# Unread products behind the transpositions of batch 0's last pair, the mix's factors loaded as rows, and w_r's second half loaded ahead of v's last pair

## The chip, the cores and the metric

One core of one Trainium2 chip runs the whole program. The metric is the device time of one execution in microseconds (us), lower is better. Before the change it is 579.75 us, the median of three runs (578.79 to 580.51).

## The reference

Three layers follow one another, in float32. A windowed attention (4 batches, 8 heads, 576 positions, head width 64; a window of 32, dilated by 4 in the upper four heads), a channel mix with a shifted input, and a mixture of four attention experts.

```python
scores = scale * np.matmul(q, k.transpose(0, 1, 3, 2))
scores = np.where(masks[None, :, :, :], scores, -1000000000.0)
attn = softmax(scores)
x = np.matmul(attn, v)                      # to [B, S, 512]
...
xk = mu_k * x + (1.0 - mu_k) * x_prev       # x_prev: x one position earlier
xr = mu_r * x + (1.0 - mu_r) * x_prev
k = np.maximum(xk @ w_k, 0.0)
v = k * k @ w_v
r = 1.0 / (1.0 + np.exp(-(xr @ w_r)))
x = r * v
...
# per expert: q, k, v = x @ wq[e], x @ wk[e], x @ wv[e]; causal softmax; @ wo[e]; top 2 of 4 summed
```

## The kernel before, in words

**Batch 0's attention.** The heads are worked in four pairs (`hp` 0 to 3). `load_qk` loads a pair's q and k, `turn_qk` turns them on TensorE (L241) and copies them out (L260 on VectorE for q, L262 on ScalarE for k). `attn_weights` makes the masked scores in two parts of five and four blocks of 64 queries (`sc`, L289 for the mask, L296), takes the rows' extreme (L309), the exponentials (L319, ScalarE) and the normalisation (L323 to L325, VectorE). `attn_values` goes over three thirds: three transpositions of the weights into a PSUM bank `pt` (L353), a copy out of it (`pts`, L354, ScalarE), then the products with v into `av` (L363). `pt` has two banks, `av` one. After four and a half blocks the result goes to the tile `x` (L378, ScalarE), which frees `av`.

**The mix.** `mix_feature` forms, for feature block f (the pair's 128 features) and each half c of the positions, `m` (L481 on ScalarE, L482 on VectorE) and splits it in a high and a low part, `xh` (L484) and `xl` (L485). The factors mu and 1-mu lie in `mus`; `load_mus` loads them with two DMAs of single 4-byte elements (L108, L109) and forms 1-mu on VectorE (L110).

**Products in three passes.** `product` (L506) multiplies high by high, low by high and high by low, so each output has 12 products (four feature blocks by three). `z` is the receptance (w_r, copied by L514), `h` the keys (w_k, L520 and after: `kh`, `kl`), `v` the values (w_v). Four output blocks fo by two halves c: `z_0_2` is c = 0, fo = 2. These share three banks (`mm`).

**Weights.** `load` fetches a part of w_r (2 parts), w_k (4) or w_v (4) raw; `split_cols` splits it: L631 (ScalarE) and L633, L634 (VectorE) on the raw words, then the high part L639 (ScalarE) and the low part L640 (VectorE). Outputs 0 and 1 of `z` need w_r's part 0, outputs 2 and 3 its part 1. Raw tiles lie in buffers of other things: w_k's part 2 and w_v's parts 1 and 3 share one buffer with the v windows (`vw`) of batch 1.

**What sets the order.** Each engine has one queue, worked front to back. A framework lays the queues out when the program is built: it follows the order of the code, but moves an instruction ahead where its own estimate says that it is ready earlier. `tc.keep_in_program_order` pins an instruction. `keep_warm` issues products of a zero tile that nobody reads (512 columns, L76), 16 at the start and one after each step of batch 0's attention. All loads named here go through one DMA queue, SP's, except pair 2's v (GpSimd's queue).

**After batch 0's attention** the layers of batch 0 start (`dbatch`: all `z`, then `h`, then `v`), and batch 1's attention is interleaved with them from about 88 us on. The later batches follow the same pattern, then the experts.

Of the kernel before, what the change touches and what calls it, by code (L numbers as in the profile page):

```python
# [8 lines left out]
F32 = mybir.dt.float32  # L9
# [12 lines left out]
def tile_dilated_attention__rwkv_channel_mix__moe_attention(  # L22
# [37 lines left out]
    def ps(tag, name):  # L60
        return psum["pool"].tile([128, 512], F32, tag=tag, name=name, bufs=psum[tag])
# [9 lines left out]
    def keep_warm(n):  # L71


        p = ps("mm", "idle")
        for _ in range(n):
            nc.tensor.matmul(p, still[:, :128], still, start=True, stop=True)  # L76

    keep_warm(16)

    def band(name, base, p1=0, j1=0):  # L80
# [4 lines left out]
        for h in range(2):  # L85
# [5 lines left out]
            if j1:  # L91
# [11 lines left out]
    nc.gpsimd.affine_select(out=tri, in_=tri, pattern=[[1, E], [-1, E]], base=-1,  # L103
                            channel_multiplier=0, compare_op=ALU.is_ge, fill=0.0)
    mus = cpool.tile([128, 2, 2, KT], F32, name="mus")

    def load_mus():
        nc.sync.dma_start(mus[:, 0, 0, :], mu_k.rearrange("(c p) -> p c", p=128))  # L108
        nc.sync.dma_start(mus[:, 0, 1, :], mu_r.rearrange("(c p) -> p c", p=128))  # L109
        nc.vector.tensor_scalar(out=mus[:, 1], in0=mus[:, 0], scalar1=-1.0, scalar2=1.0, op0=ALU.mult, op1=ALU.add)  # L110

    X = {}
# [34 lines left out]
    def load_qk(ap, dp, b, hp):  # L147

        dil = hp >= NP // 2
        qk = []
        if b == 0:
            if hp % 2 == 0:
                early["raw"] = dp.tile([128, 8, 512], F32R, tag=("wv_hi", "wv_lo")[hp // 2], name=f"rqk_{hp}",
                                       bufs=1).bitcast(F32).rearrange("p k f -> p (k f)")
            for n, src in enumerate((q, k)):
                c = 768 * (2 * (hp % 2) + n)
                r = early["raw"][:96, c : c + 768].rearrange("p (s h d) -> p s h d", h=2, s=6)
                nc.sync.dma_start(r, src[b, 2 * hp : 2 * hp + 2].rearrange("h (a s) d -> a s h d", s=6))  # L160
                qk.append(r)
            return qk
        for n, (src, nm) in enumerate(((q, "q"), (k, "k"))):
            if "rawall" not in early:
                early["rawall"] = ap.tile([128, 4, 18, 32], F32, tag="raw", name="rqk", bufs=1)
            r = early["rawall"][:, (2 * (hp % 2) if b == 1 else 0) + n]
            for j in range(2):
                for g in range(2):
                    nc.sync.dma_start(
                        r[j * 64 + g * 32 : j * 64 + g * 32 + 32],  # L170
                        src[b, 2 * hp + j].rearrange("(c t) (g e) -> g t c e", t=32, e=32)[g],
                    )
            qk.append(r)
        return qk
# [168 lines left out]
    def attn_values(ap, b, hp, vw, pe=None, pT=None):  # L343

        dil = hp >= NP // 2
        nm = f"{b}_{hp}"
        av = None
        for i in range(3):
            if pT is None:
                pt = ps("pt", f"pt_{nm}_{i}")  # L350
                pts = ap.tile([WK, 384], F32, tag="pts", name=f"pts_{nm}_{i}", bufs=2)
                for a in range(3):
                    nc.tensor.transpose(pt[:WK, 128 * a : 128 * a + 128], pe[:, 3 * i + a, :], ident)  # L353
                nc.scalar.copy(pts, pt[:WK, :384])  # L354
            for a in range(3):
                t = 3 * i + a
                cuts = [(0, 64)] if t != 4 else [(0, 32), (32, 64)]
                for u0, u1 in cuts:
                    p0 = QB * t + u0
                    if p0 in (0, 288):  # L360
                        av = ps("pt" if pT is not None and p0 else "av", f"av_{nm}_{p0}")
                    for j in range(2):
                        nc.tensor.matmul(  # L363
                            av[64 * j : 64 * j + 64, p0 % 288 : p0 % 288 + u1 - u0],
                            vw[:, j, t, :],
                            (pts[:, 128 * a + 64 * j + u0 : 128 * a + 64 * j + u1] if pT is None
                             else pT[:, 2 * j + u0 // 32 : 2 * j + u1 // 32, t, :]),
                            start=True, stop=True,
                        )
                    p1 = QB * t + u1  # L370
                    if p1 in (288, 576):
                        hf = p1 // 288 - 1
                        if dil:
                            dst = X[b][:, hp, 1 : S + 1].rearrange("p (i r) -> p r i", r=4)
                            dst, src = dst[:, 2 * hf : 2 * hf + 2, :], av[:, :288].rearrange("p (r i) -> p r i", r=2)
                        else:
                            dst, src = X[b][:, hp, 1 + 288 * hf : 289 + 288 * hf], av[:, :288]
                        nc.scalar.copy(dst, src)  # L378
            if (hp, i) == (NP - 1, 2):
                complete.add(b)  # L380
            yield

    def attn_batch(ap, dp, dq, b):
        new_x(b)
        if b == 0:

            qk = [load_qk(ap, dp, b, 0)]
            vw = [load_v(ap, b, 0)]
            qk.append(load_qk(ap, dp, b, 1))
            vw += [load_v(ap, b, 1), load_v(ap, b, 2)]  # L390
            qk += [load_qk(ap, dp, b, 2), load_qk(ap, dp, b, 3)]
            load_mus()
            load("r", 0)
            vw.append(load_v(ap, b, 3))
            load("r", 1)
            load("k", 0)
            masks_of_first(dp)
            begin_mix(dp, dq, 0, 0)
            begin_mix(dp, dq, 0, 1)
        else:  # L400
            qk, vw = [], []
        for hp in range(NP):
            with tc.issue_after(marks["v2" if hp == 0 else "window"]) if b == 1 and hp < 2 else ExitStack():
                while len(qk) < min(hp + 2, NP):
                    qk.append(load_qk(ap, dp, b, len(qk)))
                while len(vw) < min(hp + 2, NP):
                    vw.append(load_v(ap, b, len(vw)))
            yield from attn_pair(ap, b, hp, (qk[hp], vw[hp]))
            if b == 0:
                mix_feature(0, 0, 1, hp)  # L410
                mix_feature(1, 1, 1, hp)
                if hp == 0:
                    with tc.issue_after(marks["first weights"]):
                        masks_of(1)
# [198 lines left out]
    with tc.tile_pool(name="apool", bufs=2, side="left") as ap:  # L613
# [31 lines left out]
        def load(x, i):  # L645
            pool, src, kts, cols = specs[x]
            if x not in wts:
                wts[x] = tuple(pool.tile([128, kts, cols], F32R, tag=f"w{x}_{h}", name=f"w{x}_{h}") for h in ("hi", "lo"))
            raws[x, i] = load_cols(src, kts, i, {"r": "hl", "k": "3RV1", "v": "RV1V"}[x][i])
# [440 lines left out]
```

## Time and profile before

| | |
|---|---|
| runs, median of 3 | 579.75 us (578.79 to 580.51) |
| profiled execution | 577.75 us, its span 576.0 us |
| instructions | 12510 |
| TensorE (PE) busy | 546.4 us, 95% |
| VectorE (DVE) busy | 344.4 us, 60% |
| ScalarE (ACT) busy | 338.1 us, 59% |
| TensorE's granted clock, mean | 0.986 |

The profile gives, per engine, the time in which instructions ran; the granted clock is TensorE's, 1.00 for 2.4 GHz and 0.50 for 1.2 GHz. A view by stretches shows where in the span an engine is short of work; a timeline gives each instruction's start and length, and in brackets how long the engine had been idle before it and what released it. The instructions named PE are products and transpositions; SPq is the issue of DMAs on SP's queue.

### The profile page before, as it was taken

To read this page: it belongs to the slowest core of one execution; us is meant where nothing else is said; L and a number is where in the kernel's file an instruction comes from. 1 tells how busy PE (TensorE), PEld (TensorE's weight loads), DVE (VectorE), ACT (ScalarE), POOL (GpSimd) and SP (SyncE) were. 2 spreads that over 40 slices of the span, in tenths; PEclk is the share of its full clock that TensorE was granted. 3 is DMA by queue.
4 is the path that set the end of the run, shared out by engine and by line. 5 is a ranking of instruction groups with operands and counts; after the bars stand their busy time and mean duration, and the time that the engine had idled before them with its cause. 6 is when DMAs were issued, how large, how long until landed. Compare 5 with 4: busy or idle time off the path is not lost.

```text
span 576.0 us, 12510 instructions
## 1 busy us (share of the span) xinstructions
PE 546.4 (95%) x4668; PEld 490.8 (85%) x4668; DVE 344.4 (60%) x1112; ACT 338.1 (59%) x968; POOL 79.6 (14%) x101
## 2 busy tenths in 40 slices
PE   8978978899999999999999999999997999999985
PEld 4757968789999999999999999998985988989763
DVE  4567989666657388185262425428577557556662
ACT  4799978465776167285163534227566657665761
POOL 8400000000341032120011403003003003000000
PEclk9996999899999999999999999999999999999999
DMA  9987286755545553131000320054614425416202
GB/s 165 188 304 196 74 206 138 131 105 107 132 107 125 134 109 78 63 94 56 8 1 1 73 75 2 1 125 102 147 26 99 137 62 124 116 46 160 93 1 92
DMA packets 131213, 57.66 MB, mean 100 GB/s; under 512 B 110976, under 2 KB 118224, under 8 KB 131152
## 3 DMA queue, kind: packets, MB, share of 16 engines
q1 hardware_dynamic: 130736, 56.41, 41.3%
q8 instruction: 37, 0.61, 0.4%
q0 software_dynamic: 416, 0.44, 0.4%
q14 instruction: 24, 0.20, 0.1%
HBM read 34.42 MB, written 10.03 MB: 77 GB/s over the span
## 4 chain that ended last, share of the span: by engine, by line
PE 74%; DVE 9%; SPq 7%; ACT 5%; DMA 4%; issue 1%; DVEq 0%; ACTq 0%
PE v L506 17%; PE h L506 12%; PE z L506 7%; PE pv L817 5%; PE av L964 5%; PE pk L506 4%; PE pt L938 4%; PE po L1001 4%; PE pq L506 4%; PE av L363 3%; PE sc L296 3%; PE sc L891 2%; PE sc L893 2%; SPq L160 2%; SPq L182 2%
## 5 line engine op out<-in xcount | busy, mean ns | idle before, releaser
L506 PE MATMUL h<-xh,wk_hi 128*128 128x288 f32 x256 | 77.6, 304 | 4.4 <-ACT r L520 4.4
L506 PE MATMUL v<-kh,wv_hi 128*128 128x288 f32 x256 | 76.2, 302 | 0.4 <-DVE x L536 0.4
L506 PE MATMUL h<-xl,wk_hi 128*128 128x288 f32 x256 | 75.9, 297 | 0.2 <-DVE xl L485 0.2
L506 PE MATMUL v<-kl,wv_hi 128*128 128x288 f32 x256 | 75.9, 299 | 0.0
L506 PE MATMUL h<-xh,wk_lo 128*128 128x288 f32 x256 | 75.3, 294 | 0.0
L506 PE MATMUL v<-kh,wv_lo 128*128 128x288 f32 x256 | 75.3, 296 | 0.0
L903 ACT ACTIVATE pe<-pe,st 128x64 f32<-128x64 f32 (+4 forms) x80 | 44.9, 562 | 19.2 <-DVE st L897 18.0
L520 ACT ACTIVATE r<-h 128x288 f32<-128x288 f32 x64 | 25.9, 407 | 51.3 <-PE h L506 40.8
L496 POOL TENSOR_TENSOR xl<-m,xh 128x1152 fp32r<-128x1152 f32 x12 | 32.0, 2664 | 163.6 <-DMA vw<-in_v_dram 57.4
L506 PEld LDWEIGHTS h<-xh,wk_hi 128*128 128x128 f32 x256 | 48.0, 188 | 7.0 <-ACT r L520 5.6
L897 DVE CUSTOM_DVE_ANT_0 pe<-sc,cmask 128x64 f32<-128x64 f32 (+4 forms) x80 | 33.4, 427 | 31.4 <-PE sc L893 30.4
L506 PEld LDWEIGHTS v<-kh,wv_hi 128*128 128x128 f32 x256 | 48.0, 189 | 1.4 <-DVE x L536 0.6
L506 PEld LDWEIGHTS h<-xl,wk_hi 128*128 128x128 f32 x256 | 48.1, 188 | 0.8 <-DVE xl L485 0.7
L506 PEld LDWEIGHTS v<-kl,wv_hi 128*128 128x128 f32 x256 | 48.3, 189 | 0.4
L506 PEld LDWEIGHTS v<-kh,wv_lo 128*128 128x128 f32 x256 | 48.3, 189 | 0.2
L506 PEld LDWEIGHTS h<-xh,wk_lo 128*128 128x128 f32 x256 | 48.2, 188 | 0.0
L482 DVE SCALAR_TENSOR_TENSOR m<-x,mus,m 128x288 f32<-128x288 f32 x64 | 30.3, 509 | 27.1 <-ACT m L481 27.0
L319 ACT ACTIVATE pe<-pe,st 128x96 f32<-128x96 f32 x108 | 39.1, 364 | 5.8 <-DVE st L315 5.7
L536 DVE SCALAR_TENSOR_TENSOR x<-z,v 128x288 f32<-128x288 f32 x32 | 14.3, 453 | 43.5 <-PE v L506 43.4
L730 POOL TENSOR_TENSOR yl<-x,yh 128x576 fp32r<-128x576 f32 x16 | 21.0, 1344 | 139.1 <-ACT yh L729 73.7
L506 PE MATMUL z<-xh,wr_hi 128*128 128x288 f32 x128 | 39.3, 310 | 0.8 <-ACT z L514 0.8
L530 DVE TENSOR_TENSOR kl<-r,kh 128x288 fp32r<-128x288 f32 x48 | 31.7, 663 | 12.9 <-ACT kh L528 12.6
(176 smaller groups left out, 1473.6 us busy)
## 6 DMA issues: line engine op xcount, KB each, us to landing
kk<-kh SPq DMA_DIRECT2D x32, 144.0 KB, 2.6
kl<-kl SPq DMA_DIRECT2D x32, 144.0 KB, 2.7
raw_in_moe_w_k_dram<-in_moe_w_k_dram SPq DMA_DIRECT2D x4, 1024.0 KB, 9.9
raw_in_moe_w_v_dram<-in_moe_w_v_dram SPq DMA_DIRECT2D x4, 1024.0 KB, 5.8
out_dram<-ob SPq DMA_DIRECT2D x16, 256.0 KB, 2.7
rqk<-in_q_dram SPq DMA_DIRECT2D x48, 72.0 KB, 2.9
rqk<-in_k_dram SPq DMA_DIRECT2D x48, 72.0 KB, 2.7
moved<-turned SPq DMA_DIRECT2D x8, 432.0 KB, 3.1
```

The costliest lines, as they stand in the source:

```text
L319: nc.scalar.activation(pe[:, t, :], pe[:, t, :] if b else sc[:, c0 : c0 + WK], AF.Exp, bias=st[:, 0, t : t + 1], scale=-1.0, accum_out=st[ ...
L482: nc.vector.scalar_tensor_tensor(out=m, in0=x, scalar=mus[:, 0, w, f : f + 1], in1=m, op0=ALU.mult, op1=ALU.add)
L496: nc.gpsimd.tensor_sub(lo, m, hi.bitcast(F32))
L506: nc.tensor.matmul(o, w[:, kt, wsl], x[:, kt, :], start=(n == 0), stop=(n == last))
L520: nc.scalar.activation(r, p, AF.Relu)
L530: half.tensor_sub(kl[:, fo, :], r, kh[:, fo, :].bitcast(F32))
L817: nc.tensor.matmul(p, x[:, kt, t0 : t0 + tn], w[:, kt, 512:772], start=(n == 0), stop=(n == 3 * KT - 1))
L897: nc.vector.tensor_tensor_reduce(out=pe[:tn, PO[t] + c0 : PO[t] + c1], in0=sc, in1=m, scale=-0.125, scalar=(BIG if i == 0 else st[:tn, 1, ...
L903: nc.scalar.activation(pb, pb, AF.Exp, bias=st[:tn, 0, t : t + 1], scale=-1.0, accum_out=st[:tn, 2, t : t + 1])
L938: nc.tensor.transpose(pt[:kn, c0 : c0 + tn], pe[:tn, PO[t] + k0 : PO[t] + k0 + kn], ident[:tn, :tn])
L964: ins = nc.tensor.matmul(av1[p0 : p0 + 64, q0 - 64 : 512], vh[:kn, kb, :], w[i][:kn, c0 : c0 + S - q0], start=(kb == 0), stop=(kb == NB - 1))
L1001: nc.tensor.matmul(p, x[:, t0 : t0 + tn], w[:, g, :], start=(n == 0), stop=(n == 5))
```

## The change

Four edits. `keep_warm_in` issues unread products of 128 columns into the last quarter of the `pt` bank, pinned: eight behind each copy out of `pt` in batch 0's last pair, and sixteen behind that pair's last products. `load_mus` now loads both factors as eight rows of 128 elements, on ScalarE's DMA queue and at the program's head; `turn_mus` turns them on TensorE (into an `av` bank), copies them on VectorE and forms 1-mu. w_r's second half is loaded right behind its first, ahead of v's pair 3.

```diff
+    def keep_warm_in(p, n):
+        for _ in range(n):
+            tc.keep_in_program_order(nc.tensor.matmul(p[:, 384:512], still[:, :128], still[:, :128], start=True, stop=True))
...
     mus = cpool.tile([128, 2, 2, KT], F32, name="mus")
+    rows = cpool.tile([2 * KT, 128], F32, name="rows")
 
     def load_mus():
-        nc.sync.dma_start(mus[:, 0, 0, :], mu_k.rearrange("(c p) -> p c", p=128))
-        nc.sync.dma_start(mus[:, 0, 1, :], mu_r.rearrange("(c p) -> p c", p=128))
+        for w, mu in enumerate((mu_k, mu_r)):
+            nc.scalar.dma_start(rows[KT * w : KT * w + KT, :], mu.rearrange("(c p) -> c p", p=128))
+
+    def turn_mus():
+        p = ps("av", "mus")[:, : 2 * KT]
+        nc.tensor.transpose(p, rows, ident[: 2 * KT, : 2 * KT])
+        nc.vector.tensor_copy(mus[:, 0], p.rearrange("p (w c) -> p w c", w=2))
         nc.vector.tensor_scalar(out=mus[:, 1], in0=mus[:, 0], scalar1=-1.0, scalar2=1.0, op0=ALU.mult, op1=ALU.add)
...
                 nc.scalar.copy(pts, pt[:WK, :384])
+                if (b, hp) == (0, NP - 1):
+                    keep_warm_in(pt, 8)
...
             if (hp, i) == (NP - 1, 2):
                 complete.add(b)
+                if b == 0:
+                    keep_warm_in(pt, 16)
...
+            load_mus()
             qk = [load_qk(ap, dp, b, 0)]
+            turn_mus()
...
-            load_mus()
             load("r", 0)
+            load("r", 1)
             vw.append(load_v(ap, b, 3))
-            load("r", 1)
             load("k", 0)
```

The edits also change the framework's estimates, and with them the queues far behind the edited code. Three places follow.

TensorE's queue where batch 0's last pair ends and its receptance begins (`av_3_288` are the pair's products for the positions from 288 on, `z_0_0` to `z_0_2` the receptance's first outputs). Before:

```order
L363 MATMUL av_3_0_761<-pts_3_1_776,vw_3_251 64x32 x2
L363 MATMUL av_3_288_786<-pts_3_1_776,vw_3_251 64x32 x2
L363 MATMUL av_3_288_786<-pts_3_1_776,vw_3_251 64x64 x2
L363 MATMUL av_3_288_786<-pts_3_2_794,vw_3_251 64x64 x6
L506 MATMUL z_0_0_848<-xh_0_0_276,wr_hi 128x288
L506 MATMUL z_0_0_848<-xl_0_0_277,wr_hi 128x288
```

Now:

```order
L524 MATMUL z_0_2_925<-xh_0_0_280,wr_lo 128x288
L524 MATMUL z_0_2_925<-xh_0_0_280,wr_hi 128x288
L378 MATMUL av_3_288_806<-pts_3_1_788,vw_3_257 64x32 x2
L378 MATMUL av_3_288_806<-pts_3_1_788,vw_3_257 64x64 x2
L378 MATMUL av_3_288_806<-pts_3_2_814,vw_3_257 64x64 x6
L82 LDWEIGHTS still
L82 MATMUL pt_3_2_813<-still 128x128
```

Eleven of the receptance's products, the first of them `z_0_0<-xh_0_0,wr_hi`, now stand ahead of `av_3_288`, and the sixteen unread ones behind it.

ScalarE's queue at the same place (`x<-av_3_0` and `x<-av_3_288` are the copies of the pair's results, the second CAST `wr_hi` is w_r's part 0). Before:

```order
L354 COPY pts_3_2_794<-pt_3_2_793 96x384
L378 COPY x_211<-av_3_0_761 128x2x144
L639 CAST wr_hi<-raw_in_moe_w_r_dram_249 128x4x256
L484 CAST xh_0_0_276<-m_0_0_275 128x288
L378 COPY x_211<-av_3_288_786 128x2x144
L481 ACTIVATE m_0_0_275<-x_211,mus 128x288 x2
L484 CAST xh_0_0_276<-m_0_0_275 128x288
L484 CAST xh_1_1_278<-m_0_0_275 128x288
L481 ACTIVATE m_0_0_275<-x_211,mus 128x288
L484 CAST xh_1_1_278<-m_0_0_275 128x288
L631 ACTIVATE raw_in_moe_w_k_dram_269<-raw_in_moe_w_k_dram_269 128x1024
```

Now:

```order
L657 CAST wr_hi<-raw_in_moe_w_r_dram_253 128x4x256
L502 CAST xh_0_0_280<-m_0_0_279 128x288
L393 COPY x_212<-av_3_0_773 128x2x144
L499 ACTIVATE m_0_0_279<-x_212,mus 128x288
L393 COPY x_212<-av_3_288_806 128x2x144
L502 CAST xh_1_1_282<-m_0_0_279 128x288
L499 ACTIVATE m_0_0_279<-x_212,mus 128x288
L502 CAST xh_0_0_280<-m_0_0_279 128x288
L499 ACTIVATE m_0_0_279<-x_212,mus 128x288
L532 ACTIVATE z_0_891<-z_0_0_892 128x288
L532 ACTIVATE z_0_891<-z_0_1_906 128x288
L649 ACTIVATE raw_in_moe_w_k_dram_674<-raw_in_moe_w_k_dram_674 128x1024
```

The copy `x<-av_3_0` now stands behind w_r's part 0, and the first work on w_k behind the copies of `z_0_0` and `z_0_1`.

TensorE's queue where batch 0's keys end and its values begin (`h_1_7` is the last of the keys, `pt_0_0` the transpositions of batch 1's first pair). Before:

```order
L506 MATMUL h_1_7_1468<-xh_1_3_995,wk_lo 128x288
L353 MATMUL pt_0_0_1349<-ident,pe_0_1285 96x128 x3
L353 MATMUL pt_0_1_1380<-ident,pe_0_1285 96x128 x3
L363 MATMUL av_0_0_1355<-pts_0_0_1350,vw_1274 64x64 x3
L353 MATMUL pt_0_2_1396<-ident,pe_0_1285 96x128 x3
L353 MATMUL pt_1_0_1506<-ident,pe_1_1442 96x128 x3
L506 MATMUL v_0_0_1519<-kh_0_1013,wv_hi 128x288
```

Now:

```order
L524 MATMUL h_1_7_1512<-xl_1_3_1040,wk_hi 128x288
L524 MATMUL h_1_7_1512<-xh_1_3_1039,wk_lo 128x288
L524 MATMUL v_0_0_1563<-kh_0_1057,wv_hi 128x288
L524 MATMUL v_0_0_1563<-kl_0_1058,wv_hi 128x288
L524 MATMUL v_0_0_1563<-kh_0_1057,wv_lo 128x288
L524 MATMUL v_0_0_1563<-kh_0_1057,wv_hi 128x288
```

Twenty-one products of `v_0_0` now follow `h_1_7` directly; batch 1's `pt_0_0` comes behind them, and its `av_0_0` behind another 24 value products. On ScalarE the copy of `h_1_5` (L520), which frees a bank of `mm`, moves from behind the second pair's nine exponentials to ahead of them; on VectorE `kl_0_7` moves ahead of that pair's normalisation.

## Rows read from the trace of the kernel before

**Rows 1.** The page's head: span, and busy time of each engine.

```profile
span 576.0 us, 12510 instructions
PE 546.4 (95%) x4668; PEld 490.8 (85%) x4668; DVE 344.4 (60%) x1112; ACT 338.1 (59%) x968; POOL 79.6 (14%) x101
```

**Rows 2.** Windows: stretch, busy us per engine, granted clock (PEclk), DMA share, GB/s.

```profile
36.00:40.00 4.00, 1.74 (x30) 1.38 (x30) 2.45 (x7) 3.70 (x20) 0.00 (x0) 1.00 1.05 393
...
44.00:48.00 4.00, 2.23 (x30) 1.98 (x29) 3.21 (x4) 3.80 (x7) 0.00 (x0) 0.50 1.03 305
...
64.00:68.00 4.00, 4.00 (x32) 4.00 (x31) 4.00 (x7) 4.00 (x10) 0.00 (x0) 1.00 0.41 119
...
100.00:104.00 4.00, 1.28 (x10) 0.64 (x8) 3.42 (x12) 3.56 (x15) 0.00 (x0) 0.89 0.59 133
104.00:108.00 4.00, 4.00 (x24) 3.95 (x24) 2.19 (x5) 1.90 (x5) 0.00 (x0) 0.69 1.20 191
...
280.00:320.00 40.00, 40.00 (x328) 39.53 (x327) 15.65 (x31) 17.89 (x38) 8.03 (x3) 1.00 0.00 1
```

**Rows 3.** Timeline, 17 to 28 us: SP's queue, VectorE, TensorE, ScalarE.

```profile
17.80 1.99 SPq L108 DMA_DIRECT2D mus<-in_moe_mu_k_dram  x1
19.83 0.76 SPq L109 DMA_DIRECT2D mus<-in_moe_mu_r_dram  x1
...
24.60 0.17 DVE L110 TENSOR_SCALAR mus<-mus 128x8 f32<-128x8 f32 x1 [1.94 <-DMA mus<-in_moe_mu_r_dram]
...
26.83 0.65 DVE L309 TENSOR_REDUCE st<-sc 128x5 f32<-128x480 f32 x1
...
24.06 1.04 PE L296 MATMUL sc<-kT,qT 64*64 64x96 f32 x20
...
24.87 0.53 ACT L481 ACTIVATE m<-x,mus 128x288 f32<-128x288 f32 x1 [1.22 <-DVE mus L110]
```

**Rows 4.** Timeline of ScalarE, the last pair's end.

```profile
7.78 1.18 ACT L262 COPY kT<-kt 128x384 f32<-128x384 f32 x2 [5.69 <-PE kt L241]
...
40.29 0.47 ACT L354 COPY pts<-pt 96x384 f32<-96x384 f32 x1 [0.46 <-PE pt L353]
...
45.90 1.14 ACT L639 CAST wr_hi<-raw_in_moe_w_r_dram 128x1024 fp32r<-128x1024 f32 x1
...
47.56 0.70 ACT L378 COPY x<-av 128x288 f32<-128x288 f32 x1 [0.20 <-PE av L363]
...
51.84 1.20 ACT L631 ACTIVATE raw_in_moe_w_k_dram<-raw_in_moe_w_k_dram 128x1024 f32<-128x1024 f32 x1
```

**Rows 5.** Timeline of TensorE: batch 0's last pair and the receptance.

```profile
32.50 1.04 PE L76 MATMUL idle<-still 128*128 128x512 bf16 x4
...
42.45 0.91 PE L363 MATMUL av<-pts,vw 96*64 96x64 f32 x12 [0.85 <-ACT x L378]
...
46.18 1.33 PE L363 MATMUL av<-pts,vw 96*64 96x32 f32 x20 [1.76 <-ACT x L378]
...
48.09 0.44 PE L506 MATMUL z<-xh,wr_hi 128*128 128x288 f32 x1
48.34 0.44 PE L506 MATMUL z<-xl,wr_hi 128*128 128x288 f32 x1
```

**Rows 6.** Timeline of TensorE, keys to values; then ScalarE, VectorE and SP's queue there.

```profile
99.49 0.71 PE L353 MATMUL pt<-ident,pe 128*96 128x128 f32 x5
...
101.11 0.32 PE L353 MATMUL pt<-ident,pe 128*96 128x128 f32 x1 [0.91 <-DVE pe L325]
...
103.57 0.47 PE L363 MATMUL av<-pts,vw 96*64 96x64 f32 x2 [0.86 <-DMA vw<-in_v_dram]
...
105.14 0.59 PE L506 MATMUL v<-kh,wv_hi 128*128 128x288 f32 x1
...
102.71 0.41 ACT L520 ACTIVATE r<-h 128x288 f32<-128x288 f32 x1
...
103.06 0.45 DVE L530 TENSOR_TENSOR kl<-r,kh 128x288 fp32r<-128x288 f32 x1
```

## The prediction

> **What bounds the kernel now.** Start with the page's head [rows 1]: TensorE is busy 95% of 576.0 us, the two other engines under 60%. So the end moves only where TensorE is short of work or slow. The windows [rows 2] show where: from 280 to 320 us it is busy 40.00 of 40, so nothing is to be had there, while 36 to 40 us has 1.74 of 4, 44 to 48 us 2.23 at a granted clock of 0.50 (1.2 GHz), and 100 to 104 us 1.28. Between these, at 64 to 68 us, VectorE and ScalarE are both busy 4.00 of 4: there they set the pace, and a delay of theirs is passed on. The timelines then tell what TensorE waits for: around 25 us the factors of the mix [rows 3], from 40 to 52 us ScalarE's queue [rows 4, 5], from 99 to 105 us batch 1's attention [rows 6].
>
> All sums are made against the profiled execution, 577.75 us (span 576.0 and 1.75 around it). The median of the runs, 579.75, is 2.00 above it; I carry the difference over to that median. A difference under 0.3% (1.74 us) can't be told from none here.
>
> **Part 1, the factors as rows.** Removed: two DMAs of single elements, 1.99 and 0.76 us of SP's queue [rows 3]. Every later SP transfer moves up by some 2.7 us; w_r's second half also moves past the 13 transfers of v's pair 3, which then come one w_r transfer later than that. None of these is waited for: the pair's products at 42.45 wait for ScalarE, not for a DMA [rows 5]. So the moved half itself counts 0; that cover would be gone only if the pair ran many us earlier. Added: two issues on ScalarE's queue (no row shows one; from 0 to SP's 1.99 each), hidden in the 5.69 us for which ScalarE is idle before 7.78 [rows 4]; a transposition of 8 columns, and one small copy on VectorE like L110's 0.17, both about 7 to 9 us, where VectorE still waits for the first scores. Together 0.
>
> What goes is the wait: VectorE stood 1.94 us and ScalarE 1.22 us for the factors [rows 3]. Late next are the scores of pair 2: their products end at 25.10 (24.06 + 1.04), but VectorE's reduction L309, queued behind the mix, starts only at 26.83. Bounds: 0, if ScalarE's queue is held there otherwise, and 1.73. ScalarE is nearly always busy from there to 40 us, so the shift should be passed on: I take **-1.6**.
>
> **Part 2, the unread products.** Four of 512 columns took 1.04 us at the full clock [rows 5], so 0.065 for 128 columns. At 1.2 GHz two receptance products of 288 columns start 0.25 apart (48.09, 48.34), so 0.11 for 128. Bounds are 0.065 and 0.25; I take 0.11, since the stage runs at 0.50. The Trainium skill (TensorE: Matmul & The Clock Gate, "Back-to-back issue gap") gives about 81 ns for a 128-column product with its weight load; by it, an estimate, sixteen would be 1.3 us instead of the 1.8 below; no row of the kernel before has such a product.
>
> The three groups of eight (0.9 us each) lie in TensorE's waits of 0.85 and 1.76 us [rows 5] and cost 0; without that cover they would cost 2.6. But they stand behind ScalarE's copy out of the same bank and can't start before it. Do they hold the clock? In the rows it was still 1.00 from 36 to 40 us, when TensorE was busy 1.74 of 4, and 0.50 by 44 [rows 2]. The first group follows the copy that begins at 40.29 [rows 4], so the empty stretch ahead of it stays empty. I take it that the clock falls as before and comes back somewhat earlier. The Trainium skill (PSUM — Partial Sum Buffer, "PSUM bank collisions raise a hardware error") forbids TensorE to write into a bank while another engine reads it, disjoint columns included; no row shows it by itself. By that rule the free part of the bank is no place to work during the copy, and the sum is the forecast's; without it the products would fill the copies' time too, and the sum would lie towards the first rival's.
>
> **Part 3, the order at the pair's end.** Here the queues of the change matter. Today ScalarE copies `x<-av_3_288` at 47.56 [rows 4]. Now eleven receptance products stand on TensorE ahead of `av_3_288`; the first waits for w_r's part 0, whose cast ended at 47.04 (45.90 + 1.14) and now comes one copy (0.5) sooner, 46.6. Eleven by 0.25 make 49.3, `av_3_288` at its 1.33 [rows 5] 50.6: the copy comes 3.0 us later (at the full clock, 11 by 0.122, as 328 in 40 us [rows 2], and half of 1.33: 48.6, 1.0 later). Queued behind it on ScalarE are the rest of the mix and, behind the copies of `z_0_0` and `z_0_1`, the first work on w_k. These wait for sixteen unread products (1.8) and 21 of the receptance (2.6 to 5.2), so 4.4 to 7.0 after `x`; ScalarE's own steps to there take about as long as now from 47.56 to the mix's end at 51.84, 4.3. Added wait 0.1 to 2.7; I take 0.9, because the clock should return in this stretch. As ScalarE and VectorE are full later [rows 2], this is passed on: **+3.9** (bounds +1.1 and +5.7).
>
> **Part 4, the order at 99 to 107 us.** Today TensorE finishes the keys at 99.5, then stands behind batch 1's transpositions and products: it waits for the normalisation (0.91), later for `vw` (0.86), and begins the values only at 105.14 [rows 6]. It loses 2.72 us of the window from 100 to 104 (4 - 1.28), and at a mean clock of 0.69 another 1.24 from 104 to 108 [rows 2]: 3.96 us. Now 21 products of `v_0_0` follow the keys directly, 2.6 us at 0.122, and the transpositions follow when their data is there. `v_0_0` needs a free bank, today freed by L520 at 102.71, now ahead of nine exponentials; and its last three products need `kl_0_7`, today 103.06 [rows 6], now ahead of a normalisation. Bounds: 0, if these come no earlier, and -3.96. I take **-3.6**, near the far end, since both releases come sooner and the 2.6 us of products cover the rest of the way; 0.4 is left for a short wait.
>
> Sum: -1.6 + 3.9 - 3.6 = **-1.3 us**: 576.45 for the profiled execution, **578.45** on the runs' scale. That is no change that can be told.
>
> **The rivals.**
>
> *The clock stays up, or returns before the receptance starts.* For it: 24 products more in a stretch with only a few us of waits. Against it: the emptiest part lies ahead of the first group. Then part 3 costs 1.0 for the copy and some 0.4 behind it: -1.6 + 1.4 - 3.6 = -3.8, **575.95**.
>
> *Slower: part 4 gives nothing.* The values' first products wait on TensorE for a bank and `kl_0_7` as long as it waits now for batch 1's attention, because VectorE, full before 104 us (3.42 of 4 even there), delivers both late. Place: TensorE's queue behind `h_1_7`. It decides if `kl_0_7` comes more than 2.6 us behind the keys' end; each us beyond costs one, up to 3.96. Then -1.6 + 3.9 = +2.3, **582.05**. For it: the low parts come late in VectorE's queue today. Against it: both were moved ahead of 2 to 3 us of other work.
>
> *Later waits.* The queues are laid out anew up to some 300 us; batch 2's products now stand ahead of some of batch 1's receptance. If TensorE waits there for the weights' way through memory, 1 to 2 us come on top: about **580**. Against it: TensorE waits for nothing in such stretches now [rows 2].
>
> *The delay of part 3 is absorbed* by VectorE's and ScalarE's short waits between 76 and 100 us: -5.2, **574.55**. Against it: both are full before.
>
> **How the numbers follow.** Forecast 0.47, its own range 577.0 to 580.1 (part 3 from +2.4 to +5.5); clock held 0.23; part 4 gives nothing 0.17; later waits 0.09; absorbed 0.04. The range 575.3 to 581.7 takes in the first, most of the second and the fourth, and half of the third. Faster than 578.0: nearly all of the second and fifth case and four tenths of the forecast, 0.42. Slower than 581.5: most of the third, a little of the others, 0.16. The rest is 0.42.
>
> **What would show it.** Right: the wait for the factors is gone and pair 2's reduction starts near 25.1; the granted clock is near 0.50 when the receptance starts; ScalarE is idle two or three us before `x<-av_3_288`; TensorE goes from keys to values without a gap over 0.5 us, and the clock doesn't fall there. Wrong: a clock of 1.00 from 44 to 48 us; a wait of TensorE ahead of `v_0_0`'s last products; a wait over 1 us between 110 and 300 us.

## The result and the profile after

The changed kernel takes **583.81 us**, median of four runs (583.01 to 583.86), beside 579.50 for the kernel before (578.79 to 580.51) on the same chip: ratio **1.0056, 95% interval 1.0038 to 1.0075**. It is slower by 3.2 us (2.2 to 4.3), more than the 0.3% that can be told from no change. The forecast was 578.45, range 575.3 to 581.7. The profiled execution took 583.01 (span 581.3).

The page's head, against [rows 1]:

```profile
span 581.3 us, 12598 instructions
PE 553.7 (95%) x4706; PEld 495.9 (85%) x4709; DVE 346.0 (60%) x1113; ACT 337.7 (58%) x968; POOL 79.6 (14%) x101
```

TensorE is busy 7.3 us longer, so this is not only idle time: the 40 unread products are some 2.6 us of it (an estimate from the starts in the section on the prediction: eight at 0.107 us, 32 at 0.055), and some of its work ran slower or later. The windows, columns as in [rows 2]:

```profile
36.00:40.00 4.00, 1.85 (x37) 1.51 (x36) 2.58 (x6) 3.48 (x19) 0.00 (x0) 1.00 1.05 402
40.00:44.00 4.00, 4.00 (x37) 3.10 (x38) 3.05 (x6) 3.41 (x6) 0.00 (x0) 0.57 0.96 323
44.00:48.00 4.00, 2.70 (x34) 2.34 (x32) 3.66 (x4) 3.80 (x7) 0.00 (x0) 1.00 1.11 345
48.00:52.00 4.00, 4.00 (x55) 3.77 (x54) 2.13 (x6) 2.33 (x5) 0.00 (x0) 1.00 0.84 188
52.00:56.00 4.00, 4.00 (x31) 3.80 (x30) 1.19 (x3) 3.28 (x7) 0.00 (x0) 1.00 0.62 140
...
92.00:96.00 4.00, 2.52 (x43) 2.09 (x41) 1.57 (x4) 0.00 (x0) 0.00 (x0) 1.00 0.77 197
96.00:100.00 4.00, 2.17 (x10) 2.17 (x11) 3.69 (x15) 3.65 (x10) 0.00 (x0) 0.78 0.47 77
100.00:104.00 4.00, 4.00 (x46) 3.84 (x46) 3.58 (x18) 4.00 (x18) 0.00 (x0) 0.79 0.54 89
```

Three things stand out. The granted clock is 1.00 from 44 to 48 us, where it was 0.50. TensorE is full from 48 to 56 us, but VectorE does only 3.32 us of work in these eight; in the same two windows of the kernel before it did more than twice that:

```profile
48.00:52.00 4.00, 4.00 (x19) 4.00 (x18) 3.06 (x8) 3.12 (x8) 0.00 (x0) 0.51 0.76 171
52.00:56.00 4.00, 3.42 (x26) 3.18 (x25) 3.90 (x7) 4.00 (x8) 0.00 (x0) 1.00 0.68 154
```

And ScalarE does nothing at all from 92 to 96 us; after that the clock falls, while the gap of [rows 2] from 100 to 104 us is filled. The stretch from 92 to 108 us as a whole, before and now:

```profile
92.00:108.00 16.00, 12.72 (x110) 11.57 (x109) 12.29 (x44) 13.17 (x48) 0.00 (x0) 0.89 0.69 117
```

```profile
92.00:108.00 16.00, 12.69 (x130) 11.98 (x129) 12.84 (x59) 11.62 (x46) 0.00 (x0) 0.89 0.63 128
```

TensorE is short of work as long as before: the gap has moved, it has not gone.

The pair's end in ScalarE's timeline, against [rows 4]:

```profile
40.59 0.47 ACT L367 COPY pts<-pt 96x384 f32<-96x384 f32 x1 [0.62 <-PE pt L366]
...
45.70 1.18 ACT L657 CAST wr_hi<-raw_in_moe_w_r_dram 128x1024 fp32r<-128x1024 f32 x1
...
47.06 0.73 ACT L393 COPY x<-av 128x288 f32<-128x288 f32 x1
...
49.44 0.69 ACT L393 COPY x<-av 128x288 f32<-128x288 f32 x1 [0.36 <-PE av L378]
...
53.85 1.13 ACT L649 ACTIVATE raw_in_moe_w_k_dram<-raw_in_moe_w_k_dram 128x1024 f32<-128x1024 f32 x1
```

The copy `x<-av_3_0` stands behind the cast of w_r's part 0 and starts at 47.06; TensorE needs the bank that it frees. So `x<-av_3_288` starts at 49.44 (47.56 in [rows 4]) and the first work on w_k at 53.85 (51.84). The same stretch in TensorE's timeline, against [rows 5]:

```profile
41.77 1.06 PE L82 MATMUL pt<-still 128*128 128x128 bf16 x8
...
45.91 0.61 PE L82 MATMUL pt<-still 128*128 128x128 bf16 x8 [0.88 <-ACT pts L367]
...
46.93 0.40 PE L524 MATMUL z<-xh,wr_hi 128*128 128x288 f32 x1 [0.42 <-ACT wr_hi L657]
...
48.59 0.80 PE L378 MATMUL av<-pts,vw 96*64 96x32 f32 x20
49.32 1.07 PE L82 MATMUL pt<-still 128*128 128x128 bf16 x16
```

Eleven receptance products lie between 46.93 and 48.59, at the full clock. The second place is the end of the keys. First SP and ScalarE, then TensorE:

```profile
88.61 0.44 SPq L640 DMA_DIRECT2D raw_in_moe_w_v_dram<-in_moe_w_v_dram  x1
...
91.41 0.45 ACT L541 ACTIVATE kh<-r 128x288 fp32r<-128x288 f32 x1
96.31 1.17 ACT L649 ACTIVATE raw_in_moe_w_v_dram<-raw_in_moe_w_v_dram 128x1024 f32<-128x1024 f32 x1 [4.46 <-DMA raw_in_moe_w_v_dram<-in_moe_w_v_dram]
97.38 0.69 ACT L538 ACTIVATE r<-h 128x288 f32<-128x288 f32 x2
```

```profile
97.83 0.40 PE L524 MATMUL h<-xh,wk_hi 128*128 128x288 f32 x1 [3.21 <-ACT r L538]
...
105.93 0.29 PE L524 MATMUL h<-xh,wk_lo 128*128 128x288 f32 x1
106.06 0.29 PE L524 MATMUL v<-kh,wv_hi 128*128 128x288 f32 x1
```

SP issues w_v's part 3 at 88.61, and ScalarE's first step on it stands ahead of two copies of the keys. ScalarE stands 4.46 us for the transfer, TensorE 3.21 us for the copies. The last key product starts at 105.93 and the first value product at 106.06: no gap, but 0.92 us later than the 105.14 of [rows 6].

### The profile page after: what moved, and what is told of

Read it like the earlier page. It is cut to its first block, busy times and chain, and to the rows that moved or that the text cites. A ratio compares the mean times of both kernels' runs of the same rounds, so it can differ in the third digit from the quotient of the medians.

```text
span 581.3 us, 12598 instructions
## 1 busy us (share of the span) xinstructions
PE 553.7 (95%) x4706; PEld 495.9 (85%) x4709; DVE 346.0 (60%) x1113; ACT 337.7 (58%) x968; POOL 79.6 (14%) x101
## 4 chain that ended last, share of the span: by engine, by line
PE 82%; DVE 6%; ACT 4%; DMA 3%; SPq 2%; issue 2%; DVEq 0%; ACTq 0%
PE v L524 16%; PE h L524 15%; PE z L524 8%; PE pv L835 5%; PE av L982 5%; PE sc L309 4%; PE pk L524 4%; PE pt L956 4%; PE po L1019 4%; PE pq L524 4%; PE av L378 4%; PE sc L909 2%; PE sc L911 2%; PE idle L76 2%; PE pt L366 1%
## 5 line engine op out<-in xcount | busy, mean ns | idle before, releaser
L524 PE MATMUL h<-xh,wk_hi 128*128 128x288 f32 x256 | 79.3, 311 | 6.0 <-ACT r L538 5.9
L524 PE MATMUL h<-xl,wk_hi 128*128 128x288 f32 x256 | 77.2, 302 | 2.3 <-DVE xl L503 2.3
L524 PE MATMUL h<-xh,wk_lo 128*128 128x288 f32 x256 | 76.7, 300 | 0.6 <-DVE wk_lo L658 0.6
L524 PEld LDWEIGHTS h<-xl,wk_hi 128*128 128x128 f32 x256 | 49.5, 193 | 2.8 <-DVE xl L503 2.7
L524 PEld LDWEIGHTS h<-xh,wk_lo 128*128 128x128 f32 x256 | 49.5, 193 | 0.8 <-DVE wk_lo L658 0.8
L956 PE MATMUL pt<-ident,pe 128*128 128x128 f32 (+1 forms) x240 | 35.4, 275 | 3.8 <-DVE pe L936 3.4
```

What stands on the lines that cost most here:

```text
L524: nc.tensor.matmul(o, w[:, kt, wsl], x[:, kt, :], start=(n == 0), stop=(n == last))
L956: nc.tensor.transpose(pt[:kn, c0 : c0 + tn], pe[:tn, PO[t] + k0 : PO[t] + k0 + kn], ident[:tn, :tn])
```

## The experiments

Twelve kernels, each timed beside the kernel before on the same chip (its medians: 580.55 for the first four, 579.69 for the next four, 580.26 for the three after, 580.52 for the last). Comparisons go by the ratios:

| kernel | ratio, 95% interval | median us |
|---|---|---|
| e1 products only | 1.0054 (1.0034 to 1.0073) | 583.12 |
| e2 factors as rows only | 0.9929 (0.9909 to 0.9949) | 576.89 |
| e3 w_r's move only | 1.0009 (0.9987 to 1.0032) | 580.97 |
| e4 change, w_v's part 3 two steps later | 1.0086 (1.0067 to 1.0105) | 585.52 |
| e5 change, four products each, none at the end | 1.0045 (1.0026 to 1.0065) | 581.39 |
| e6 change, four products each and sixteen | 1.0065 (1.0038 to 1.0091) | 583.34 |
| e7 change, the sixteen only | 1.0018 (0.9996 to 1.0041) | 580.43 |
| e8 change, no products | 0.9953 (0.9929 to 0.9976) | 576.91 |
| e9 as e8, the copy made late | 1.0048 (1.0027 to 1.0069) | 583.24 |
| e10 change, the copy made early | 0.9912 (0.9887 to 0.9937) | 575.15 |
| e11 as e10, no products | 0.9941 (0.9918 to 0.9965) | 576.48 |
| e12 before, the copy made early | 0.9950 (0.9929 to 0.9971) | 577.54 |

### The change in its parts: e1, e2, e3

e1 is the kernel before with this, and `keep_warm_in`:

```diff
                 nc.scalar.copy(pts, pt[:WK, :384])
+                if (b, hp) == (0, NP - 1):
+                    keep_warm_in(pt, 8)
...
                 complete.add(b)
+                if b == 0:
+                    keep_warm_in(pt, 16)
```

> Only the unread products (8, 8, 8 and 16), the factors and w_r loaded as before. Three theories of the 3 to 4 us that the whole change lost. Queue theory: ScalarE's queue stands still for w_v's part 3 (4.46 us in the changed kernel) with r_0_6 and r_1_4 behind it, TensorE waits 3.2 us for that and then runs slow; the order there is the same with the products alone, so 583 to 584.5 us, with an idle ScalarE of over 3 us near 92. Pair theory: the copy of av_3_288 and the first work on w_k come 2 us later and this is passed on; that order is the same here too, so about 582.5, with or without the wait. Head theory: the factors' turning delays the first scores by 1.1 us; without it the first copy of kT is back at 7.8 and the time is at 582.5 or less.

Measured: 1.0054, all of the change's loss. The head theory falls: the copy of kT is back in its place (7.95), and the loss remains. The order of the compute engines is that of the change from 40 us on, so this run doesn't separate the other two. In its profile (of a run of 586.77 us) ScalarE waited 4.95 us for w_v's part 3, and the granted clock was 0.50 from 44 to 52 us, not 1.00, with the same products in the same order.

e2 has only the other new part, `load_mus` and `turn_mus` as in the change's diff, with `load("r", 1)` in its old place.

> Only the factors as rows, w_r loaded as before, no unread products. The order at the pair's end stays that of before (av_3_288 ahead of the receptance), while the queues behind 60 us are laid out anew. Queue theory: w_v's part 3 stands ahead of one copy of the keys fewer, and is waited for less if its load is earlier; 578 to 581. Pair theory: nothing is delayed at the pair's end, so 579.5 less what the wait for the factors gave, down to 577.9. Head theory: 1.1 us more at the head, first copy of kT at 8.9, and 580.6 or more.

Measured: 0.9929, a gain of 4.1 us, where the prediction had 1.73 at most from this part. The copy of kT is at 7.95 here too, with the rows: most of the 1.1 us of the head theory was the slow start of one profile (the last section).

e3 swaps two lines:

```diff
-            vw.append(load_v(ap, b, 3))
             load("r", 1)
+            vw.append(load_v(ap, b, 3))
```

> Only w_r's second half ahead of v's pair 3. No compute engine's order changes, SP's queue alone. All theories: no change, 579.5 within 0.9; a loss would show at the pair's first products (42.45 before), if they came to wait for v's pair 3.

Measured: 1.0009, no difference. This part is done with.

### The wait for w_v: e4

```diff
-"v3": 42}
+"v3": 44}
```

> The whole change, with the split of w_v's part 3 placed two steps later in the table of steps, so that the copies r_0_6 and r_1_4 and their squares stand ahead of it on ScalarE. Queue theory: TensorE's 3.2 us before a product of the keys near 95 shrink to under 1, the clock stays up there, and the time falls to 579 to 580.5. Pair theory: what the pair's end lost stays lost and ScalarE waits for something else; 582.5 to 584. Head theory: 583 to 584.

Measured: 1.0086, against the queue theory, and above the pair theory's 582.5 to 584 too. What TensorE waited for up to 120 us, and ScalarE from 60 to 112 (total, times, longest):

```profile
PE sc L309 <- DVE kT L282: 2.2, 1, 2.2
PE h L524 <- ACT r L538: 2.2, 1, 2.2
...
ACT raw_in_moe_w_v_dram L649 <- DMA raw_in_moe_w_v_dram<-in_moe_w_v_dram: 2.3, 3, 1.5
```

The wait for w_v is down from 5.7 us in all to 2.3 and the longest from 4.5 to 1.5, but in its place TensorE waits 2.2 us for VectorE's `kT`. I read this as an earlier delay that comes to light at one wait or the other, neither being its source. Why this kernel is no faster than the change, and rather slower, although TensorE waits less up to 120 us, stays open.

### Whose queues, whose pair's end: e5 to e8

The partial kernels fall into groups. The pair's end has two orders: the copy `x<-av_3_0` ahead of the cast of w_r's part 0 (early, as before) or behind it (late, as in the change). The queues from 60 us on have three: those of the kernel before, those of the rows alone, and those of the change. Other numbers of products give other pairs of these.

```diff
-                if (b, hp) == (0, NP - 1):
-                    keep_warm_in(pt, 8)
+                if (b, hp) == (0, NP - 1) and (4, 4, 4)[i]:
+                    keep_warm_in(pt, (4, 4, 4)[i])
...
-                if b == 0:
-                    keep_warm_in(pt, 16)
```

That is e5; e6 leaves the sixteen in; e7 takes the groups of eight out and leaves the sixteen; e8 takes all out.

> The whole change with four unread products instead of eight behind each copy, and none behind the pair's last products. The pair's end stays as in the change (ten receptance products ahead of av_3_288), but the queues behind it are those of the kernel with the rows alone, which took 0.9929 of the time of before. Layout theory: what the whole change lost lies in the queues behind 60 us (w_v's part 3 waited for on ScalarE); here 576.5 to 578.5 us, ScalarE waiting under 2 us for w_v. Pair theory: the later copy of av_3_288 and the later start on w_k (51.8 before, 53.9 in the change) are passed on through the full stretch to 76 us; 579 to 581.

> As the kernel with four each, with the sixteen behind the pair's last products again: the pair's end is that of the change, the queues behind 60 us are nearly those of before (TensorE stands again behind batch 1's transpositions at 100 us). Layout theory: no change from before, 579 to 581. Pair theory: 2 us later than before, 582 to 583.5.

> The rows and w_r's move, and the sixteen products behind the pair's last ones alone: the pair's end and all queues are nearly those of before, but the factors come as rows. It tells what the rows themselves give. If the gain of the rows alone (0.9929) lies in the wait for the factors and the shorter SP queue, 576 to 577.5 here; if it lies in the queues that they re-laid at 100 us (TensorE went from keys to values without a gap), 579 to 581, with TensorE short of work from 100 to 104 us as before.

> The whole change without any unread product: rows and w_r's move. Both theories: the time of the rows alone, 0.993 of before (576 to 577.5), since w_r's move alone gave 1.0009 and moves nothing else in the order. If the two add up to something else, 578 or more.

Put into one table (ratios to the kernel before):

| queues from 60 us on | copy early | copy late |
|---|---|---|
| of the kernel before | 1 (before), 1.0018 (e7) | 1.0065 (e6) |
| of the rows | 0.9953 (e8), 0.9929 (e2) | 1.0045 (e5) |
| of the change | none | 1.0056 (change), 1.0054 (e1) |

The late copy costs 0.0047 with the queues of before (2.7 us, e6 against e7, whose intervals touch) and 0.0092 with those of the rows (5.3 us, e5 against e8). Both pairs differ in twelve products too, and a little in the order behind the pair's end: e6 and e7 up to 72 us, e5 and e8 from 94 to 112 us. With the copy late, all three sets of queues give the same within their intervals; e4, with a fourth set, lies above them. The pair theory stands; the layout theory is right only about where the gain of e2 comes from. e7 shows that gain's other side: rows, but queues of before, and nothing is gained.

The profiles of e8 and e5, whose first transposition is at 6.88 in both, show where the 5.3 us arise. ScalarE in e5 (e8's rows follow in the next section); then a wait of TensorE in the keys and VectorE's last step on batch 0, in e8 and in e5:

```profile
51.08 0.68 ACT L393 COPY x<-av 128x288 f32<-128x288 f32 x1 [0.92 <-PE av L378]
...
55.32 1.20 ACT L647 ACTIVATE raw_in_moe_w_k_dram<-raw_in_moe_w_k_dram 128x1024 f32<-128x1024 f32 x1
```

```profile
73.63 0.40 PE L520 MATMUL h<-xl,wk_hi 128*128 128x288 f32 x1 [0.78 <-DVE xl L499]
...
143.47 0.46 DVE L550 SCALAR_TENSOR_TENSOR x<-z,v 128x288 f32<-128x288 f32 x1 [2.22 <-PE v L520]
```

```profile
76.90 0.40 PE L522 MATMUL h<-xl,wk_hi 128*128 128x288 f32 x1 [0.78 <-DVE xl L501]
...
147.39 0.46 DVE L552 SCALAR_TENSOR_TENSOR x<-z,v 128x288 f32<-128x288 f32 x1 [2.22 <-PE v L522]
```

In e5 `x<-av_3_288` is 3.24 us later (51.08 against 47.84), the first work on w_k 3.21 (55.32 against 52.11), TensorE in the keys 3.27 (76.90 against 73.63), and the last `x<-z,v` of batch 0 3.9 (147.39 against 143.47); the spans of these two profiles differ by 3.7. So the delay arises at the pair's end and is passed on whole, through a stretch in which the two kernels have the same order; the different order from 94 us on adds 0.6 at most.

### The copy's place without products: e9

That leaves the twelve products. So e8 got one edge: the copy is issued behind the cast (`marks["hi"]`, w_r's part 0).

```diff
...
-                        nc.scalar.copy(dst, src)
+                        with tc.issue_after(marks["hi"]) if (b, hp, hf) == (0, NP - 1, 0) else ExitStack():
+                            nc.scalar.copy(dst, src)
...
```

> No unread product at all; rows and w_r's move as in the kernel without products (0.9953 of before, 576.9 us), and one edge that puts the copy x<-av_3_0 behind the cast of w_r's part 0 on ScalarE, as in the change. TensorE's queue then has ten receptance products ahead of av_3_288; all queues behind 60 us stay those of the kernel without products. Order theory (the loss is the place of this copy): 580 to 582, as the kernel with four products each (581.4). Products theory (the loss is the products' own time, the waits that their bank brings, or the clock): 576 to 577.5.

Measured: 1.0048, 583.24 us, a little above the order theory's range. The products theory falls: without one unread product the late copy costs 0.0095, 5.5 us (1.0048 less 0.9953). ScalarE's timeline of e8, then of e9:

```profile
45.71 0.69 ACT L391 COPY x<-av 128x288 f32<-128x288 f32 x1
46.18 1.15 ACT L653 CAST wr_hi<-raw_in_moe_w_r_dram 128x1024 fp32r<-128x1024 f32 x1
...
47.84 0.70 ACT L391 COPY x<-av 128x288 f32<-128x288 f32 x1 [0.18 <-PE av L376]
...
52.11 1.21 ACT L645 ACTIVATE raw_in_moe_w_k_dram<-raw_in_moe_w_k_dram 128x1024 f32<-128x1024 f32 x1
```

```profile
45.75 1.11 ACT L654 CAST wr_hi<-raw_in_moe_w_r_dram 128x1024 fp32r<-128x1024 f32 x1
46.76 0.67 ACT L392 COPY x<-av 128x288 f32<-128x288 f32 x1
...
50.87 0.67 ACT L392 COPY x<-av 128x288 f32<-128x288 f32 x1 [0.81 <-PE av L376]
...
55.12 1.20 ACT L646 ACTIVATE raw_in_moe_w_k_dram<-raw_in_moe_w_k_dram 128x1024 f32<-128x1024 f32 x1
```

The copy `x<-av_3_0` moves by 1.05 us. By then ten receptance products can start, TensorE's queue has them first, and at the clock of 0.50 to 0.68 there they hold `av_3_288` up: `x<-av_3_288` comes 3.03 us later, and the first work on w_k 3.01. Meanwhile VectorE has little to do, as in the change:

```profile
48.00:52.00 4.00, 4.00 (x36) 3.65 (x36) 1.46 (x4) 2.06 (x4) 0.00 (x0) 0.68 0.72 163
52.00:56.00 4.00, 2.75 (x19) 2.30 (x17) 2.25 (x5) 2.30 (x5) 0.00 (x0) 1.00 0.83 186
56.00:60.00 4.00, 1.67 (x7) 1.67 (x8) 3.24 (x6) 4.00 (x10) 0.00 (x0) 0.67 0.01 2
```

VectorE does 3.71 us of work from 48 to 56 us (e8: 6.95). TensorE then runs dry from 56 to 60 us and the clock falls once more, to 0.50 from 60 to 64 us. In e5 it did not (1.00 there). e5 has e9's order on every compute engine, from the first instruction to the last, and twelve unread products besides: 1.0045 and 1.0048, so over the runs neither these products nor that fall of the clock shows.

### The copy early: e10, e11, e12

The other way round: in the whole change the cast of w_r's part 0, and the subtraction behind it, are issued behind the copy.

```diff
...
+        part_hi, part_lo, w = when_late["r0"]
+        with tc.issue_after(marks["x030"]):
+            nc.scalar.copy(part_hi, w)
+        nc.vector.tensor_sub(part_lo, w, part_hi.bitcast(F32))
         mixes[0] = [mixing[n][1:] for n in range(2)]
```

(`marks["x030"]` is the copy `x<-av_3_0`; `conv("r", 0)` stores its last two steps in `when_late`.) e11 is the same without products, e12 the same edge on the kernel before.

> The whole change with all 40 unread products, but the cast of w_r's part 0 issued behind the copy x<-av_3_0, by one edge: no receptance product stands ahead of av_3_288, and some of w_k's split moves ahead on ScalarE and VectorE. The queues behind 60 us are nearly those of the kernel without products. Order theory: 575 to 577.5. Products theory: 580 to 582.

> The same edge (w_r's part 0 cast behind x<-av_3_0) without any unread product; w_k's split starts earlier on ScalarE. Order theory: the products neither help nor hurt, so within 0.3% of the kernel with them and the same edge, 575 to 577. If the clock that the products hold up in the receptance is worth something, this one is 1 us or more slower than that one.

> The kernel before, with nothing of the change in it, but the edge that puts the cast of w_r's part 0 behind the copy x<-av_3_0. Its queues behind 60 us come out as those of the kernels with the rows. Order theory: the rows themselves are worth nothing and the gain of 0.5 to 0.9% lies in the queues, so 0.993 to 0.996 of before here too (576 to 577.5). If the rows' shorter SP queue and the saved wait for the factors carry that gain, this one takes 579 or more.

Measured: 0.9912, 0.9941, 0.9950. e10 holds every edit of the change and all 40 products, and **beats both kernels**: 0.9% under before, 1.4% under the change (1.0056 less 0.9912). Its timeline of ScalarE:

```profile
45.55 0.68 ACT L393 COPY x<-av 128x288 f32<-128x288 f32 x1
46.03 1.11 ACT L712 CAST wr_hi<-raw_in_moe_w_r_dram 128x1024 fp32r<-128x1024 f32 x1
47.05 1.15 ACT L649 ACTIVATE raw_in_moe_w_k_dram<-raw_in_moe_w_k_dram 128x1024 f32<-128x1024 f32 x1
...
48.52 0.70 ACT L393 COPY x<-av 128x288 f32<-128x288 f32 x1
```

The first work on w_k is at 47.05 instead of 53.85. In these three kernels the edge also moved w_k's split ahead, so they are not a pure test of the copy. e9 against e8 is the nearest: up to 94 us all that differs is the place of the copy, with what it moves on the engines up to 54 us; behind 94 us not quite all queues are those of e8, as the expectation had it, but those of e5. e12 has the factors still loaded element by element and w_r in its old place, yet its queues come out as those of e11, from 40 us on instruction for instruction. e11 has the rows and w_r's move: 0.9941 against 0.9950. The change and e1 are such a pair too (1.0056 with the rows, 1.0054 without). So the rows by themselves are worth nothing that can be measured; the queues behind them are. e10 and e11 differ by 0.0029 with overlapping intervals; whether the products are worth anything stays open.

## Why the prediction was wrong

**Part 1 (−1.6): the step "the shift should be passed on" failed.** The waits for the factors did go. But from 10 to 30 us VectorE now waits 5.2 us for the scores (4.8 before) and 2.2 for ScalarE's `xh` (0.4 before): other things were due next. e2, whose first transposition is as early as that of before (6.14 and 6.11), shows the shift shrink: pair 2's reduction starts 1.5 us earlier (25.32 against 26.83), the next one 1.0 (28.35 against 29.34), the last pair's first copy 0.4 (39.89 against 40.29). In the change it is even 0.3 later (40.59), behind a slow start (the last section). With the queues of before the rows gave 1.0018 (e7, lower end 0.9996): not −1.6 but nothing that can be measured. My bounds, 0 and 1.73, held this; I took the far end. SP's later transfers did not all move up by 2.7 us either: the 13 of v's pair 3 now take 13.18 us to issue, 8.65 before, and the loads of w_k behind them begin at 33.04 instead of 30.99. No engine waited for a load between 15 and 60 us.

**Part 2 (0): right in the sum, for another reason than I gave.** The sixteen took 0.88 us to the next product's start at the full clock (49.32 to 50.20), 0.055 each; the eight of the first group, at the low clock, start 0.107 apart (41.775 to 42.523). I had 0.11 for all, which is the low clock's figure. The Trainium skill (TensorE: Matmul & The Clock Gate, "Back-to-back issue gap") gave 81 ns, each of these products having a weight load of its own here too; the trace says 55 at the full clock, and decides. The third group waited 0.88 us for the copy out of its bank, as I had it; none worked beside a copy, so what the Trainium skill (PSUM — Partial Sum Buffer, "PSUM bank collisions raise a hardware error") says of such a collision no run here shows. e10 with all 40 products is the fastest kernel, and with the copy late the change (1.0056, 40 products) and e9 (1.0048, none) agree within their intervals, so no cost of the products themselves shows.

"I take it that the clock falls as before" was wrong in this profile (1.00 from 44 to 48) and right in others: with all 40 products the granted clock of that window was 1.00 in the change and e4, 0.50 in e1 and e10. And it did not decide. The fastest kernel, e10, ran at 0.50 from 40 to 48 us; the change ran at 1.00 from 44 on and lost. With the late copy the clock does show at the pair's end, where ScalarE waited 2.17 us for `av_3_288` in e1 and 0.36 in the change, yet the two kernels take the same time (1.0054 and 1.0056).

**Part 3 (+3.9, from 1.1 to 5.7): right in place and sign, and in size within its bounds.** In the profile `x<-av_3_288` is 1.9 us later (I had 3.0 at the low clock and 1.0 at the full one), the first work on w_k 2.0: the wait that I added between the two, 0.9, was 0.1. Alone, the late copy costs 2.7 us with the queues of before and 5.3 to 5.5 with those of the rows. It has less to hide behind there, because those queues have no gap at 100 us that takes up a delay; that is my reading of e5 and e6, not a run by itself. What I had not seen is what passes it on: the mix goes back and forth between ScalarE and VectorE, and the late copy leaves VectorE idle for over half of 48 to 56 us just ahead of the stretch of [rows 2] in which it is full.

**Part 4 (−3.6): the step that decided, and it failed.** TensorE does go from keys to values without a gap, as said, but the gap only moved: from 92 to 108 us it is busy 12.69 us, and was busy 12.72 before. But I took the gain from the place where the gap had been, and left out what now stood ahead of it: the keys' last product starts at 105.93, 6.6 us later than the 99.36 of before, as ScalarE waits for w_v's part 3 with two copies of the keys behind it. Its load was issued 2.3 us later than before (88.61, 86.33 before), with the pair's end 1.9 late ahead of it. That order stood in ScalarE's queue ahead of the rows that I had read. The price itself was about right: where the queues give it and the copy is early, the gain is 2.7 us (e8) and 4.1 (e2), two measures of one order, and TensorE is busy there for 15.60 and 15.85 us of 16 (e8, then e2):

```profile
92.00:108.00 16.00, 15.60 (x178) 14.73 (x176) 14.03 (x64) 13.12 (x53) 0.00 (x0) 1.00 0.68 118
```

```profile
92.00:108.00 16.00, 15.85 (x177) 15.10 (x174) 13.50 (x63) 13.11 (x53) 0.00 (x0) 1.00 0.70 122
```

How much of the gain the late copy takes away in the change's own queues, and how much w_v's place in them, no run separates.

So, as far as the runs tell, the sum should have read 0 + 2.7 + 0, as in the queues of before, whose gap the change keeps in another place; measured is +3.2 (2.2 to 4.3). In the queues of the rows it reads 0 + 5.3 − 2.7 = 2.6, which is e5 (1.0045). Parts 3 and 4 can't be priced one without the other. The rival "part 4 gives nothing" had the right total, 582.05, with a wrong mechanism: nothing waited for a bank or for `kl_0_7`. "The clock stays up" came true as to the clock of the change's profile and brought none of its gain. Of the signs, "a clock of 1.00 from 44 to 48" did come; "a wait over 1 us between 110 and 300" did not (TensorE is busy 189.74 of these 190 us). Of the signs of being right, the clock did not hold between keys and values: it was 0.78 and 0.79 from 96 to 104 us.

Not tried: the change's own queues from 60 us on with the copy early. The edge that makes it early (e10) also laid those queues out anew, so how much the wait for w_v costs by itself stays open.

## What to carry to other kernels

An instruction that costs nothing where it stands can still move what a scheduler puts behind it: read the whole changed order from the edit to the end, and on every engine ask which instruction came to stand ahead of a release (here a 1.1 us cast ahead of the copy that frees a bank). A gain priced at one place holds only if everything ahead of it arrives on time, so follow the chain back from there before adding it to the sum. Build the parts of a change one by one and sort them by the orders that they give: here kernels that shared the compute engines' order behind the last pair shared their time to within the noise, whatever the edit was (before, e3 and e7: 1, 1.0009, 1.0018; e2 and e8: 0.9929, 0.9953; e5 and e9: 1.0045, 1.0048; the change and e1: 1.0056, 1.0054; e11 and e12: 0.9941, 0.9950).

## What the runs showed of the hardware

The start of the same code is not always equally fast. The first rows of TensorE's timeline, before and after:

```profile
1.26 5.02 PE L76 MATMUL idle<-still 128*128 128x512 bf16 x16 [1.26 <-DVE still L69]
```

```profile
1.26 5.99 PE L76 MATMUL idle<-still 128*128 128x512 bf16 x16 [1.26 <-DVE still L69]
```

Over the fourteen profiles of this study the first transposition starts anywhere from 6.05 to 7.14 us, with the same sixteen products ahead of it. Their weight loads are 0.43 us apart at first, and closer from 4.2 us on before, from 5.9 on in the change; the windows show a granted clock of 1.00 all the while. The Trainium skill (TensorE: Matmul & The Clock Gate, "Part 1: The HAM clock gate") says that the number of such slow products at a kernel's start changes from run to run, and the trace agrees. So up to 1 us between two single profiles can be this alone, and up to 1.0 us of the 5.3 between the two spans. It is not always passed on: e12 starts 0.89 us later than the kernel before (7.00 against 6.11), finds the factors' load further along (a wait of 0.87 us instead of 1.94), and has the last pair's first copy at 40.13, no later than the 40.29 of before.

The second such place is near 440 us. Both kernels leave TensorE short of work there in the same three waits (1.10, 0.77 and 0.90 us). From 420 to 460 us the granted clock was 1.00 in the kernel before and in e2, and 0.91 to 0.96 in the other twelve profiles. What that can do to two single profiles shows in e2 and e8, which have one order on all compute engines: their spans are 572.9 and 576.0. Of the 3.1 us, 0.7 are there at the start; 2.4 come in between 434 and 439 us, where the clock was 1.00 in e2 and fell to 0.66 in e8 (mean of 430 to 440).
